# One copy instead of six of the logit and gate columns in a routed two-layer kernel

## The chip, the cores and the metric

The kernel runs on one core of one Trainium2 chip. The metric is the time of one execution on the device in microseconds (us). The engines are named as the profile names them: PE is TensorE, PEld its weight loads, DVE is VectorE, ACT is ScalarE, POOL is GpSimd and SP is SyncE, which issues most of the transfers.

## The reference

A gated scan over 4 x 5056 tokens of 256 features comes first, then two mixture-of-experts layers with 8 experts of width 1024. Layer 1 has a skip score for every token.

```python
f = lower_bound + (1 - lower_bound) * sigmoid(f_logit)
h = f[:, t] * h + (1 - f[:, t]) * x[:, t]            # the scan; its outputs are the tokens x
logits = x @ w_gate                                  # 8 columns for each layer
e = argmax(logits); g = softmax(logits)[e]
y = g * (relu(x @ w1[e]) @ w2[e])                    # for the tokens of expert e
out = x + y where x @ w_skip > 0, else x             # layer 1
out = y                                              # layer 2, on layer 1's output
```

## The kernel before

**Stages.** The 20224 tokens are cut into 40 chunks of 512 (the last is shorter), and each chunk into tiles of 128. For each chunk the kernel loads x and f (lines 818 to 829), makes the gates on ACT (lines 834 and 839), scans on DVE (lines 844 and 856), transposes the result back to rows on PE (line 880, copied out of PSUM by ACT at line 883), computes the logits (function `logits`, from line 894), routes, ranks, and scatters the rows into a region for each expert in DRAM. From the 17th chunk on (I0 = 16) units of up to 256 tokens of layer 1 run in between, four steps to a chunk: two products (lines 609 and 637 to 639) with the results split in two float16 halves by ACT (line 620) and DVE (line 621). When the scan is through, the remaining units of layer 1 and then those of layer 2 follow, one after the other.

**The logits.** One matrix `wgt` of 17 columns holds both layers' gates and the skip vector. For the first 20 chunks (CF = 20) `logits` multiplies in float32: for each of 4 tiles and each of 2 halves of the features, the transposed tokens are the stationary operand, loaded anew each time, and `wgt17` is the moving one. `wgt17` is `wgt` read RG times over through a broadcast view, so that a product streams 6 x 17 = 102 columns and fills 102 columns of PSUM; only the first 17 are read afterwards, by ACT at line 916. Later chunks use float16 halves with 34 and 17 columns (lines 923 and 926) and no copies.

**The gate products.** Layer 1's second weights are extended by 8 columns, the product of the expert's `w2` with layer 2's gate. `wsplit` transposes a quarter of a weight on PE (line 1029, copied out by ACT at line 1030), and `gate_product` (line 1032) makes 4 x 2 float32 products with the transposed quarter stationary and `wgt8`, 8 columns read RG times, moving: 48 columns, of which 8 are read by ACT and DVE in `w_split` (lines 184 and 185). There are 16 such batches (8 experts, two quarters each), and they all lie in the first 127 us. The same function is called in `reload`, which belongs to a loop for units left over at the end.

**What sets the order.** Each engine's order is written out by hand: `side(k)` calls `work`, `weights` and the unit steps slot by slot, and PE, DVE, ACT, POOL and SP keep that order. In the trace a float32 product is two matmul instructions, so a batch of logits for one chunk and a batch of gate products for one quarter are 16 each; a transpose is one. The logits of a chunk go to PSUM tiles that they share with the transposes of line 880 (pool `pt`, 2 buffers of one size for all), so that a batch waits for ACT's copy at line 883.

Of the kernel before, what the change touches and what calls it, by code (L numbers as in the profile page):

```python
# [56 lines left out]

WB, LT, LT2, UW = 2, 6, 5, 4

RG = 6  # L60
CLG, CTOK, CGATE = D, D + E, D + E + 1
W = 272

# [31 lines left out]
def moe_chain(ctx: ExitStack, tc: tile.TileContext, xT, fT, lb, wg, w1a, w2a, w1b, w2b, out):  # L95
# [74 lines left out]

    wgt17 = wgt.unsqueeze(2).broadcast_to([P, 2, RG, 17])
    wgt8 = wgt[:, :, :E].unsqueeze(2).broadcast_to([P, 2, RG, E])

# [568 lines left out]
    with ExitStack() as ph:  # L742
# [152 lines left out]
        def logits(c):  # L895
# [8 lines left out]
            if c < CF:  # L904
                psl = pt.tile([P, CJ, RG, 17], F32, tag="px", name="ps_l")
                for j in range(n):
# [125 lines left out]
        def gate_product(wT):  # L1032

            psv = pm.tile([P, 4, RG, E], F32, tag="pm", name="ps_v")
            for f in range(4):
# [485 lines left out]
```

## Time and profile before

| | us |
|---|---|
| median of 3 runs | 1583.88 |
| lowest and highest | 1580.51 and 1587.67 |
| profiled execution | 1587.33 |
| its span, first to last instruction | 1585.6 |
| PE busy in it | 1498.6 (95%) |
| DVE busy, ACT busy | 925.5 (58%), 725.0 (46%) |
| mean granted PE clock | 0.979 |

Busy shares are averages over stages with different limits, so the stretches are to be read one by one. The granted clock stands beside each stretch: 1.00 is 2.4 GHz and 0.50 is 1.2 GHz; a value in between is a mean over a stretch with both. In the timeline an instruction's own time is longer than the distance to the next, since matmuls are pipelined: the pace is read from the starts.

### The profile page before, as it was taken

The numbers are of one execution on the slowest core, as the hardware profiler recorded it, in microseconds if no ns is written. First come the engines' busy times: TensorE is split into PE (matmuls) and PEld (weight loads), VectorE is DVE, ScalarE is ACT, GpSimd is POOL, SyncE is SP. The second block draws the span as 40 slices with busy tenths as digits, with TensorE's granted clock in tenths as the row PEclk, the third lists the DMA queues.
The fourth block names the chain that finished last, engine by engine and source line by source line (L and its number), as shares of the span: only waits on it lengthen the run. The fifth ranks groups of instructions, "written<-read, shape, count | busy, mean of one in ns | idle before, by whom it ended". The sixth has DMA issues, their size and how long they took to land. (4 is left out here: it accounts for less than half of the span.)

```text
span 1585.6 us, 41240 instructions
## 1 busy us (share of the span) xinstructions
PE 1498.6 (95%) x13900; PEld 1346.4 (85%) x13901; DVE 925.5 (58%) x1947; ACT 725.0 (46%) x1419; POOL 507.9 (32%) x511
## 2 busy tenths in 40 slices
PE   5878989999999998999999999999999999999996
PEld 5877868888988887887888998998989989989985
DVE  5877677888885865546755555544444444444442
ACT  6777567776763232333344443433333333333332
POOL 1663455646453177016111111111111111111121
PEclk9988989999999999999999999999999999999998
DMA  8876655777774377327333323111111111111110
GB/s 289 274 266 212 212 178 201 260 243 252 242 253 153 103 232 244 121 71 243 110 100 103 97 98 106 50 49 56 49 50 57 47 51 50 49 54 49 49 48 22
DMA packets 127221, 213.73 MB, mean 135 GB/s; under 512 B 14459, under 2 KB 87807, under 8 KB 124464
## 3 DMA queue, kind: packets, MB, share of 16 engines
q1 hardware_dynamic: 107824, 157.51, 31.5%
q0 software_dynamic: 19200, 53.53, 9.2%
q8 instruction: 132, 2.16, 0.6%
q14 instruction: 65, 0.53, 0.1%
HBM read 120.10 MB, written 70.80 MB: 120 GB/s over the span
## 5 line engine op out<-in xcount | busy, mean ns | idle before, releaser
L621 DVE SCALAR_TENSOR_TENSOR hl<-ps_m,hh 128x512 f16<-128x512 f32 (+1 forms) x504 | 336.9, 668 | 554.6 <-ACT hh L620 553.1
L620 ACT ACTIVATE hh<-ps_m 128x512 f16<-128x512 f32 (+1 forms) x504 | 292.2, 580 | 634.8 <-PE ps_m L609 527.3
L637 PE MATMUL ps_o<-wt,hh 128*128 (+2 forms) x1936 | 531.7, 275 | 8.4 <-DVE rows L645 8.4
L638 PE MATMUL ps_o<-wt,hh 128*128 (+2 forms) x1936 | 531.8, 275 | 0.0
L639 PE MATMUL ps_o<-wt,hl 128*128 (+2 forms) x1936 | 531.7, 275 | 0.0
L609 PE MATMUL ps_m<-xh,w1s 128*128 128x256 f16 (+1 forms) x2880 | 505.9, 267 | 0.0
L609 PEld LDWEIGHTS <-w1s 128*128 128x128 f16 x4320 | 406.7, 98 | 45.5 <-issue 0.4
L274 POOL DMA_INDIRECT out_dram<-rows,dest x162 | 157.6, 973 | 750.1 <-ACT rows L681 636.8
L609 PE MATMUL ps_m<-xl,w1s 128*128 128x256 f16 (+1 forms) x1440 | 378.6, 267 | 0.0
L638 PEld LDWEIGHTS <-hh 128*128 128x128 f16 x1936 | 190.0, 98 | 33.5 <-issue 9.3
L609 PE MATMUL ps_m<-xh,wt 128*128 128x256 f16 x1152 | 215.9, 276 | 2.4 <-DVE hl L621 2.4
L639 PEld LDWEIGHTS <-hl 128*128 128x128 f16 x1936 | 190.1, 98 | 25.0
L637 PEld LDWEIGHTS <-hh 128*128 128x128 f16 x1936 | 190.0, 98 | 22.6
L274 POOL DMA_INDIRECT regions<-rw,dest x158 | 175.9, 1113 | 91.9 <-issue 42.5
L609 PEld LDWEIGHTS <-wt 128*128 128x128 f16 x1728 | 168.8, 99 | 23.8 <-issue 3.1
L609 PE MATMUL ps_m<-xl,wt 128*128 128x256 f16 x576 | 158.7, 276 | 0.0
L583 DVE COPY w1s<-wt 128x4096 f16 x90 | 110.8, 1231 | 11.6 <-issue 4.8
L274 POOL DMA_INDIRECT regions<-wt,b_dest x80 | 84.7, 1059 | 42.2 <-issue 17.9
L856 DVE TENSOR_TENSOR_SCAN xt<-ft,end,xt 128x512 f32<-128x512 f32 (+4 forms) x78 | 94.9, 1246 | 0.4
L598 DVE SCALAR_TENSOR_TENSOR xl<-ps_x,xh 128x512 f16<-128x512 f32 (+1 forms) x126 | 83.1, 660 | 16.7 <-ACT xh L597 16.6
L596 PE MATMUL ps_x<-ident,rows 128*128 128x128 f32 x484 | 75.0, 276 | 18.2 <-DMA rows<-regions 18.2
L681 ACT ACTIVATE rows<-ps_o,rows 128x256 f32<-128x256 f32 x162 | 68.3, 471 | 33.2 <-PE ps_o L639 33.2
(241 smaller groups left out, 1317.1 us busy)
## 6 DMA issues: line engine op xcount, KB each, us to landing
rows<-regions SPq DMA_DIRECT2D x116, 272.0 KB, 2.8
wt<-wt SPq DMA_DIRECT2D x20, 1024.0 KB, 6.0
ft<-in_fT_dram SPq DMA_DIRECT2D x39, 512.0 KB, 4.0
xt<-in_xT_dram SPq DMA_DIRECT2D x39, 512.0 KB, 4.9
wt<-mid SPq DMA_DIRECT2D x40, 272.0 KB, 4.5
mid<-rows SPq DMA_DIRECT2D x38, 272.0 KB, 3.6
wt<-in_w2a_dram SPq DMA_DIRECT2D x16, 512.0 KB, 4.7
wt<-in_w1a_dram SPq DMA_DIRECT2D x16, 512.0 KB, 3.9
```

The source lines that it names most:

```text
L274: r = nc.gpsimd.indirect_dma_start(out=dst, out_offset=bass.IndirectOffsetOnAxis(ap=idx_ap, axis=0), in_=rows_ap, in_offset=None, bounds_c ...
L583: nc.vector.tensor_copy(t.w1, wt[:, bass.ds(o, W2O)])
L596: nc.tensor.transpose(ps[:, d, j * P : (j + 1) * P], t.rows[:, j, d * P : (d + 1) * P], ident)
L598: nc.vector.scalar_tensor_tensor(out=t.xl, in0=ps, scalar=SX, in1=t.xh, op0=ALU.mult, op1=ALU.subtract)
L609: nc.tensor.matmul(ps[:, f, :], lhsT=t.w1[:, wo : wo + P], rhs=x[:, d, :], start=f == 0 and k == 0, stop=f == 1 and k == 5, skip_group_che ...
L620: nc.scalar.activation(hh, ps, AF.Relu)
L621: nc.vector.scalar_tensor_tensor(out=hl, in0=ps, scalar=0.0, in1=hh, op0=ALU.max, op1=ALU.subtract)
L637: nc.tensor.matmul(ps, lhsT=hh[:, f, js], rhs=hi, start=first, stop=False)
L638: nc.tensor.matmul(ps, lhsT=hh[:, f, js], rhs=lo, start=False, stop=False)
L639: nc.tensor.matmul(ps, lhsT=hl[:, f, js], rhs=hi, start=False, stop=last)
L681: nc.scalar.activation(y, t.ps[j][:, :D], AF.Copy, scale=t.rows[:, j, CGATE : CGATE + 1])
L856: nc.vector.tensor_tensor_scan(x[:, d, s0:s1], f[:, d, s0:s1], x[:, d, s0:s1], init, ALU.mult, ALU.subtract)
```

## The change

RG falls from 6 to 1. The broadcast views then hold one copy: each logits product of the first 20 chunks streams 17 columns instead of 102, and each gate product 8 instead of 48. The number of matmuls, of weight loads, of copies out of PSUM and of transfers stays as it is, and so do the results, since the five further copies were never read. The PSUM tiles shrink with RG, inside pools whose buffers are sized by other tiles.

```diff
-RG = 6
+RG = 1
 CLG, CTOK, CGATE = D, D + E, D + E + 1
```

The lines that read RG, unchanged:

```python
wgt17 = wgt.unsqueeze(2).broadcast_to([P, 2, RG, 17])            # line 171
wgt8 = wgt[:, :, :E].unsqueeze(2).broadcast_to([P, 2, RG, E])    # line 172
psl = pt.tile([P, CJ, RG, 17], F32, tag="px", name="ps_l")       # line 905
psv = pm.tile([P, 4, RG, E], F32, tag="pm", name="ps_v")         # line 1034
```

## Rows read from the trace of the kernel before

**Rows 1.** Windows by stage: busy us (instructions) per engine, granted clock, DMA share.

```profile
14.64:143.11 128.47, 104.97 (x792) 100.22 (x792) 100.41 (x200) 96.90 (x204) 64.58 (x62) 0.86 0.81 270
143.11:240.00 96.89, 85.12 (x754) 75.14 (x754) 70.08 (x136) 60.70 (x111) 48.38 (x38) 0.94 0.57 187
240.00:480.00 240.00, 234.86 (x2392) 209.65 (x2391) 195.14 (x468) 170.16 (x327) 131.41 (x110) 1.00 0.70 240
...
800.00:1200.00 400.00, 400.00 (x3667) 360.15 (x3665) 196.89 (x285) 155.04 (x277) 70.01 (x72) 1.00 0.24 75
```

**Rows 2.** Groups by line, PE, 14.64 to 143.11 us: busy, mean ns, idle before.

```profile
L1037 PE MATMUL ps_v<-wgt,wt 128*128 128x48 f32 x256 | 35.6, 299 | 2.2 <-ACT wt L1030 2.2
L908 PE MATMUL ps_l<-wgt,xt 128*128 128x102 f32 x224 | 34.4, 316 | 15.3 <-ACT rw L883 15.3
L1029 PE MATMUL ps_w<-ident,wt 128*128 128x128 f32 x128 | 19.9, 307 | 0.0
L880 PE MATMUL ps_t<-ident,xt 128*128 128x128 f32 x113 | 18.0, 304 | 3.9 <-ACT rw L883 2.5 <-DVE xt L856 1.3
...
L225 PE MATMUL ps_rank<-oh,ones 128*128 128x112 f16 (+6 forms) x42 | 2.3, 192 | 0.0
```

**Rows 3.** Timeline, PE, 66 to 73 us: start, length, instructions merged by batch.

```profile
67.24 1.06 PE L1029 MATMUL ps_w<-ident,wt 128*128 128x128 f32 x8
68.13 1.93 PE L908 MATMUL ps_l<-wgt,xt 128*128 128x102 f32 x16
69.90 0.22 PE L222 MATMUL ps_rank<-oh,ltri 128*128 128x128 f16 x1
...
70.24 1.93 PE L1037 MATMUL ps_v<-wgt,wt 128*128 128x48 f32 x16
72.02 1.05 PE L1029 MATMUL ps_w<-ident,wt 128*128 128x128 f32 x8
```

**Rows 4.** Timeline, PE, 110 to 122 us.

```profile
110.47 3.74 PE L908 MATMUL ps_l<-wgt,xt 128*128 128x102 f32 x16 [1.02 <-ACT rw L883]
114.00 3.53 PE L1037 MATMUL ps_v<-wgt,wt 128*128 128x48 f32 x16
117.33 1.93 PE L1029 MATMUL ps_w<-ident,wt 128*128 128x128 f32 x8
119.05 1.51 PE L880 MATMUL ps_t<-ident,xt 128*128 128x128 f32 x8
120.40 1.88 PE L1037 MATMUL ps_v<-wgt,wt 128*128 128x48 f32 x16
```

**Rows 5.** Windows by batch, columns as in rows 1 (PE first, clock third last).

```profile
22.62:24.42 1.80, 1.80 (x16) 1.80 (x17) 1.12 (x1) 1.13 (x2) 0.00 (x0) 1.00 1.10 366
24.52:27.86 3.34, 3.34 (x19) 3.34 (x17) 2.71 (x5) 1.49 (x5) 0.00 (x1) 0.50 1.06 399
27.86:31.20 3.34, 3.34 (x17) 3.23 (x17) 2.10 (x6) 3.28 (x8) 0.22 (x1) 0.50 1.05 373
31.49:33.35 1.86, 1.86 (x16) 1.86 (x17) 1.77 (x6) 1.86 (x3) 0.00 (x0) 1.00 0.35 105
...
92.70:96.00 3.30, 3.30 (x18) 3.30 (x17) 3.10 (x5) 2.71 (x4) 2.59 (x2) 0.50 0.69 245
96.45:98.19 1.74, 1.74 (x19) 1.74 (x17) 1.29 (x6) 1.39 (x5) 0.46 (x2) 1.00 0.77 262
```

**Rows 6.** Windows from one logits batch to the next, columns as in rows 1.

```profile
41.12:49.10 7.98, 5.54 (x51) 5.31 (x50) 6.69 (x17) 6.66 (x16) 6.50 (x6) 1.00 0.83 249
...
110.47:123.01 12.54, 12.54 (x72) 12.54 (x73) 8.33 (x23) 7.55 (x17) 6.74 (x7) 0.62 0.74 246
```

**Rows 7.** Waits of ACT, 110.47 to 123.01 us: total us, times, longest.

```profile
ACT ls L916 <- PE ps_l L908: 2.9, 1, 2.9
```

**Rows 8.** Timeline, PE, 253 to 258 us: logits of a later chunk, in float16.

```profile
254.26 0.18 PE L923 MATMUL ps_l<-wg,ft 128*128 128x34 f16 x1 [0.51 <-ACT rw L883]
254.28 0.17 PE L926 MATMUL ps_l<-wg,ft 128*128 128x17 f16 x1
```

## The prediction

> **What bounds the kernel now.** I read the windows by stage first, then PE's groups in the one stage that the change touches, then PE's timeline there with the granted clock beside it. The windows [rows 1] show three regimes. From 240 us on PE is busy 234.86 of 240.00 us and later 400.00 of 400.00 us at full clock: its own order of work sets the end. From 143 to 240 us it is busy 85.12 of 96.89 us. In the first stage, 14.64 to 143.11 us, no engine is: PE 104.97, DVE 100.41, ACT 96.90 of 128.47 us, and the clock averages 0.86. Each engine's order is fixed and the units of layer 1 stand in PE's order behind this stage's work, so a microsecond that the first stage loses or gains reaches the end nearly whole, as PE has hardly an idle stretch later in which to make it up.
>
> All 256 instructions of the gate products and 224 of the logits (14 batches of 16) lie in that stage [rows 2]; the other 6 batches of logits stand after 143 us among dense float16 products.
>
> **What a narrow product costs PE.** The change removes 85 of 102 moving columns from a logits product and 40 of 48 from a gate product, and no instruction. The pace is read from the starts at full clock [rows 3]: 16 logits instructions take 69.90 - 68.13 = 1.77 us, 16 gate products 72.02 - 70.24 = 1.78 us, 8 transposes 68.13 - 67.24 = 0.89 us. That is 0.111 us an instruction for 102, 48 and 128 columns alike, so columns don't set it; each instruction has its own float32 stationary operand, and that is what these batches have in common. At half clock [rows 4] it is the same picture: 3.53 us, 3.33 us and 1.72 us, so 0.221, 0.208 and 0.215 us each. Taking 48 columns as the nearest row to 17 and 8, the removed columns save nothing on the pace. From both sides: at most the pace of a float16 product of 17 columns, which comes 0.02 us after the one before it [rows 8] (a far row with other operands; it is a rival below), and no loss, since in no row fewer columns take longer. What is saved besides is the end of a batch's last matmul: 102 columns against 48 are 316 against 299 ns in the mean [rows 2], so some 0.03 us in each of 30 batches, 1 us if all of it is waited for. ACT and DVE read the same 17 and 8 columns at another stride: nothing, with either sign too small for a row. PSUM buffers, transfers and queues are untouched, and no wait is added.
>
> **What it costs in clock.** What the removed columns did do is keep PE occupied. The windows by batch [rows 5] show what PE did before each change of level. At 22.62 us 16 logits run at 1.00 after a pause, and the clock is 0.50 from 24.5 us on. The next batch, 16 gate products without a gap, keeps PE busy 3.34 of 3.34 us and the clock stays at 0.50. Then 16 transposes of 128 columns run, equally without a gap, and from 31.49 us it is 1.00. The same order stands at 110.47 us [rows 4]: logits and gate products of 102 and 48 columns run at half for 6.86 us, 16 transposes follow, and at 120.40 us the next gate products start at the full pace. At 92.70 us a batch nearly all of logits ran at 0.50, and the next products were at 1.00 [rows 5]. So with PE equally busy, batches of 128 columns raised the clock, batches of 102 did once and once didn't, batches of 48 didn't. With 17 and 8 columns I expect that logits and gate products never raise it and that each run of them lets it fall; only runs of transposes raise it.
>
> The Trainium skill ("TensorE: Matmul & The Clock Gate", Part 1, What's actually happening) says that a monitor sets the clock by how busy PE has lately been. Read as the time that PE is busy, that rule would leave this change without any effect; the gate products at 0.50 with PE busy throughout [rows 5] speak against that reading.
>
> **The sum.** PE's work in the first stage, at either level. Full [rows 2, 3]: 256 x 0.111 + 224 x 0.111 + (128 + 113) x 0.111 = 80 us, and 6 rank batches of 70.24 - 69.90 = 0.34 us, a dozen products of the first unit and 4 transposes for 3 us more: 83 us. Half [rows 2, 4]: 256 x 0.208 + 224 x 0.221 + 241 x 0.215 = 155 us, and twice 3 us: 161 us. Today the stage takes 128.47 us, 104.97 us of it busy, so PE waits 23.5 us, mostly for ACT's copy out of PSUM before a logits batch (15.3 us [rows 2]).
>
> How much of the waiting stays: at full clock a turn from one batch of logits to the next takes 7.98 us with 5.54 us busy; a turn with a second batch of gate products (72 instructions for 51) at a mean of 0.62 takes 12.54 us, all of it busy [rows 6]. So a slow PE becomes the bound of its turn, ACT and DVE are covered by it, and ACT waits for PE instead (2.9 us in that turn, for the logits [rows 7]; the extension's copies and the transposes' copies stand behind it on ACT, and behind these the next logits). Bounds for the idle time that stays: 0 and 23.5 us. I take half, 12 us, since the stretches at full clock and the start of the stage keep theirs.
>
> Which share is at full: a turn holds one run of logits and, for most, gate products, then up to 16 transposes on end. Such a run lasts 3.5 us at half; I take it that it raises the clock by its end or shortly before, and that the next narrow run takes it away again. That leaves about 2 us in turns of some 10 to 11 us, a fifth at full, a mean clock of 0.60. The stage then takes 83 / 0.60 + 12 = 150 us, 22 us more than 128.47. Ends: half of the time at full, mean 0.75, with 12 us idle gives 123 us, no loss at all; a third at full, mean 0.67, gives 136 us, +8; everything at half gives 161 us without and 185 us with today's idle time, +33 to +56.
>
> After 143 us nothing changes: the 6 batches of logits there stand between products of 256 columns at 0.94 and 1.00 [rows 1], which are dense without them. The first unit's products at 140 us may start at half for a little longer (under 2 us, as today's batches at half cost twice), which I set against the 1 us saved above. Of the 22 us all reaches the end. On the profiled execution (1587.33 us, 1.7 us around a span of 1585.6) that is 1609; it lay 3.45 us above the median, so the forecast is 1584 + 22 = **1606 us**.
>
> **Rivals.** *The clock holds as today.* If transposes alone raise it, as before 31.49 and 120.40 us [rows 4, 5], and pauses alone lower it, PE runs the same pace at the same levels: 1584 us, within 8 us of before. For it: the pauses before logits at full clock are real (15.3 us in all [rows 2]), and falls follow them. Against it: the rise before 96.45 us, with logits ahead of it [rows 5]. Chance 0.12.
>
> *Nothing raises it.* The whole stage runs at half: 161 to 185 us, the middle 173, +44, so 1628 us. For it: where a turn has a second batch of gate products, these stand between its transposes. Against it: the two rises behind 16 transposes on end. Chance 0.15. The Trainium skill (the same page, Part 4: PE-mode transpose) says that transposes don't count as PE being busy in the same way; by that rule this rival would be the forecast, with its 1628 us. The rises after runs of transposes alone [rows 4, 5] disagree with it.
>
> *Columns are the pace after all.* If narrow float32 products came as fast as the float16 ones, 0.02 us instead of 0.111 [rows 8], PE would save about 480 x 0.09 = 43 us of its busy time in the first stage, and ACT would set the turns: its 96.90 us and some waiting, about 112 us, -16, so 1568 us. Its place is the 30 batches, and it decides if 16 narrow products at full clock take under about 1.2 us. Against it: 48 and 102 columns differ by 0.01 us in 16. Chance 0.04.
>
> **How the numbers follow.** The forecast, a clock that is at half for most of the first stage and raised by transposes only, has 0.69, from +8 to +33 us: 1592 to 1617. The clock as today 0.12, half throughout 0.15 (1617 to 1640), columns as the pace 0.04. The range takes the forecast's own and most of half throughout, 1589 to 1630; outside it lie most of the first rival, the third, and the upper end of the second, some 0.2 in all. A measurement of this kernel can tell about 0.5%, 8 us, from no change. Slower by more: 0.69 and 0.15, less a little for forecasts that end low, 0.83. Within: 0.13. Faster: 0.04.
>
> **What would show it.** In the changed kernel's windows the first stage's clock should be near 0.60 instead of 0.86, the stage some 20 us longer with PE busy over 90% of it, and everything after it the same length, moved. PE's timeline should still show 16 logits in 1.8 us at full and 3.3 to 3.5 us at half; ACT's waits for line 908 and 1037 should grow while PE's waits for line 883 shrink. I am wrong if the clock stays at 0.8 or more there, if 16 narrow products take clearly less than 3.3 us at half, or if the stage grows and the end doesn't.

## The result: 1.1% slower, all of it lost in the first stage

| | before | after |
|---|---|---|
| median of 6 runs, us | 1584.85 | 1602.63 |
| lowest and highest, us | 1579.92, 1587.67 | 1596.04, 1608.45 |
| ratio, with its 95% interval | 1 | 1.0106 [1.0074, 1.0139] |
| span of the profiled execution, us | 1585.6 | 1599.9 |
| first to fifteenth batch of logits ("the first stage"), us | 128.5 | 143.9 |
| from there to the end of the span, us | 1442.5 | 1441.5 |

The first stage is 15.4 us longer, the rest of the profiled execution 1.0 us shorter. The windows by stage of the changed kernel show it (columns: stretch, us, then PE, PEld, DVE, ACT and POOL busy with instructions, granted clock, DMA share, GB/s); rows 1 answer to them.

```profile
14.50:158.36 143.86, 136.05 (x792) 131.81 (x792) 100.54 (x200) 98.23 (x204) 65.12 (x62) 0.67 0.72 242
158.36:255.00 96.64, 88.58 (x757) 77.81 (x757) 70.43 (x138) 60.98 (x112) 47.86 (x38) 0.91 0.56 187
255.00:495.00 240.00, 235.07 (x2393) 209.56 (x2391) 195.30 (x466) 170.14 (x327) 131.33 (x110) 1.00 0.70 240
...
815.00:1215.00 400.00, 400.00 (x3666) 360.16 (x3665) 197.10 (x285) 154.54 (x276) 70.01 (x72) 1.00 0.24 75
33.30:158.36 125.06, 118.80 (x713) 115.02 (x712) 88.72 (x179) 85.99 (x180) 64.66 (x60) 0.62 0.68 229
```

PE has the same 792 instructions there and is busy 136.05 us instead of 104.97 us; DVE and ACT are busy as long as before. One thing must be known to read the clock column: until the trace's first clock record, here at 33.3 us, it shows 1.00, though the pace says half (16 logits in 17.94 - 14.50 = 3.44 us). So the last row begins there: 0.62, against 0.86 in before from 33 us to the end of its first stage (that row stands with the experiments).

The groups by line of PE in the first stage (busy, mean ns of one, idle time before them), which answer to rows 2:

```profile
L1037 PE MATMUL ps_v<-wgt,wt 128*128 128x8 f32 x256 | 46.2, 318 | 0.0
L908 PE MATMUL ps_l<-wgt,xt 128*128 128x17 f32 x224 | 37.6, 314 | 5.4 <-ACT rw L883 5.4
L1029 PE MATMUL ps_w<-ident,wt 128*128 128x128 f32 x128 | 29.0, 402 | 0.0
L880 PE MATMUL ps_t<-ident,xt 128*128 128x128 f32 x113 | 26.5, 409 | 2.4 <-ACT rw L883 2.4
```

The gate products have a sixth of their columns and take 46.2 us instead of 35.6. The transposes, of which the change touches nothing, take 29.0 + 26.5 = 55.5 us instead of 19.9 + 18.0 = 37.9. Work that was not edited grew by nearly half: that is a clock, not the cost of an instruction.

PE's timeline of the changed kernel, its pace at either level (answers to rows 3 and 4):

```profile
14.50 3.60 PE L908 MATMUL ps_l<-wgt,xt 128*128 128x17 f32 x16
17.94 1.95 PE L1029 MATMUL ps_w<-ident,wt 128*128 128x128 f32 x8
...
96.31 1.96 PE L908 MATMUL ps_l<-wgt,xt 128*128 128x17 f32 x16 [1.02 <-ACT rw L883]
98.11 0.26 PE L222 MATMUL ps_rank<-oh,ltri 128*128 128x128 f16 x1
...
98.66 3.53 PE L1037 MATMUL ps_v<-wgt,wt 128*128 128x8 f32 x16
102.04 1.95 PE L1029 MATMUL ps_w<-ident,wt 128*128 128x128 f32 x8
103.78 1.63 PE L880 MATMUL ps_t<-ident,xt 128*128 128x128 f32 x8
105.24 1.85 PE L1037 MATMUL ps_v<-wgt,wt 128*128 128x8 f32 x16
106.95 0.31 PE L1029 MATMUL ps_w<-ident,wt 128*128 128x128 f32 x1
```

At full clock 16 products of 17 columns take 98.11 - 96.31 = 1.80 us and 16 of 8 columns 106.95 - 105.24 = 1.71 us; at half 3.44 us and 102.04 - 98.66 = 3.38 us. With 102 and 48 columns it was 1.77 and 1.78 us, 3.53 and 3.33 us. The removed columns saved PE at most 0.07 us in a batch of 16.

### The profile page after: what moved, and what is told of

It is laid out like the page before. It is cut to its first block, busy times and chain, and to the rows that moved or that the text cites. A ratio compares the mean times of both kernels' runs of the same rounds, so it can differ in the third digit from the quotient of the medians.

```text
span 1599.9 us, 41241 instructions
## 1 busy us (share of the span) xinstructions
PE 1533.4 (96%) x13900; PEld 1380.4 (86%) x13901; DVE 926.1 (58%) x1947; ACT 726.3 (45%) x1419; POOL 507.7 (32%) x511
## 5 line engine op out<-in xcount | busy, mean ns | idle before, releaser
L681 ACT ACTIVATE rows<-ps_o,rows 128x256 f32<-128x256 f32 x162 | 68.3, 471 | 33.3 <-PE ps_o L639 32.9
```

Source lines behind the costliest of these rows:

```text
L681: nc.scalar.activation(y, t.ps[j][:, :D], AF.Copy, scale=t.rows[:, j, CGATE : CGATE + 1])
```

## The experiments

Two theories stood against each other at first: the clock (narrow products leave PE too little occupied, and it runs at half for longer) and the edit's other effect, a smaller PSUM tile that ACT and DVE read at another stride; further on, that narrow products cost time by themselves. Each kernel ran beside the kernel before on one chip, and chips differ by 2%, so ratios are compared, not times. The stage and the clock are those of one profiled execution each, and executions of one kernel differ, so a few microseconds of a stage decide nothing.

| kernel | ratio to before [95%] | first stage, us | clock from 33 us to its end |
|---|---|---|---|
| before | 1 | 128.5 | 0.86 |
| the changed kernel, again | 1.0125 [1.0092, 1.0158] | 145.1 | 0.60 |
| one copy, old PSUM layout | 1.0142 [1.0092, 1.0192] | 145.9 | 0.59 |
| three copies | 1.0066 [1.0040, 1.0093] | 144.1 | 0.64 |
| logits one, gates six | 1.0046 [1.0021, 1.0071] | 133.2 | 0.72 |
| logits six, gates one | 1.0022 [0.9990, 1.0054] | 138.2 | 0.76 |
| one copy, float16 products between | 1.0016 [0.9993, 1.0039] | 135.7 | 0.83 |
| logits seven, gates sixteen | 0.9970 [0.9947, 0.9993] | 127.4 | 0.91 |
| the same, and products in the pauses | 0.9958 [0.9932, 0.9984] | 124.9 | 0.97 |
| one copy, products between and in the pauses | 0.9960 [0.9934, 0.9985] | 128.5 | 0.94 |

The windows from 33 us to the end of the first stage that the last column is read from. The length of the stretch comes before the comma, PE's busy time behind it, the clock third last.

Before:

```profile
33.00:143.11 110.11, 89.24 (x700) 85.31 (x700) 87.77 (x179) 83.28 (x177) 64.12 (x60) 0.86 0.78 259
```

The changed kernel, again:

```profile
33.00:159.67 126.67, 122.47 (x711) 118.82 (x711) 88.66 (x179) 86.17 (x179) 61.48 (x60) 0.60 0.68 225
```

One copy in the old PSUM layout:

```profile
33.00:160.57 127.57, 123.03 (x700) 119.78 (x699) 87.82 (x179) 85.22 (x177) 61.22 (x60) 0.59 0.67 224
```

Three copies:

```profile
33.00:158.53 125.53, 116.84 (x714) 112.57 (x712) 88.68 (x179) 86.46 (x180) 61.45 (x60) 0.64 0.70 228
```

Logits one, gates six:

```profile
33.00:147.42 114.42, 102.44 (x709) 98.52 (x709) 88.61 (x179) 85.07 (x179) 64.71 (x60) 0.72 0.75 251
```

Logits six, gates one:

```profile
33.00:152.53 119.53, 102.33 (x702) 98.67 (x702) 88.26 (x179) 84.32 (x177) 62.73 (x60) 0.76 0.71 239
```

One copy, float16 products between:

```profile
33.00:149.94 116.94, 98.05 (x922) 94.50 (x922) 88.66 (x179) 85.08 (x178) 63.65 (x60) 0.83 0.76 247
```

Logits seven, gates sixteen:

```profile
33.00:141.89 108.89, 84.94 (x702) 80.31 (x700) 87.60 (x179) 83.12 (x177) 72.62 (x60) 0.91 0.79 264
```

The same, and products in the pauses:

```profile
33.00:141.23 108.23, 92.81 (x831) 87.32 (x829) 87.29 (x179) 82.94 (x177) 65.81 (x60) 0.97 0.79 264
```

One copy, products between and in the pauses:

```profile
33.00:145.26 112.26, 100.89 (x1042) 95.87 (x1042) 87.69 (x179) 83.33 (x177) 66.38 (x60) 0.94 0.78 256
```

**One copy in the old layout.** The matmuls write one copy; the tiles keep six.

```diff
-RG = 6
+RG = 1
-psl = pt.tile([P, CJ, RG, 17], F32, tag="px", name="ps_l")
+psl = pt.tile([P, CJ, 6, 17], F32, tag="px", name="ps_l")
-                            psl[:, j],
+                            psl[:, j, :RG],
...
```

> One copy is computed, but the PSUM tiles keep their room for six, so ACT and DVE read at the old stride. Clock theory: nothing but the moving columns matters, so it runs as the changed kernel: 1603 us (+18), the first stage (first logits batch to the fifteenth) 142 to 146 us, its clock 0.6 to 0.7. Rival, layout (the narrower PSUM tile is read or shared differently): as before, 1585 us, the stage 128 us.

Measured: 1.0142, the stage 145.9 us, the clock 0.59 (0.62 over the whole stage), as the changed kernel on another chip. With the old layout the loss is all there: the layout and the stride are not the cause.

**Each part alone.**

```diff
-RG = 6
+RL, RE = 1, 6
```

RL counts the copies of the logits' columns, RE those of the gate products'; the second run has 6 and 1.

> Only the logits are computed once; the gate products keep six copies (48 columns). Clock theory: the logits, the wider of the two, carry most of the loss, since the clock of the kernel before never rose behind gate products alone: +10 to +14 us, the first stage 138 to 143 us. Rival, equal shares (each narrow batch costs alike, 14 batches to 16): +8 us. Rival, the clock holds and something else costs: no number, but then the stage's clock stays at 0.86.

> Only the gate products are computed once; the logits keep six copies (102 columns). Clock theory: runs of logits and transposes still raise the clock or keep it, runs of gate products let it fall a little more often than before: +3 to +8 us, the first stage 131 to 137 us. Rival, equal shares: +9 us.

Measured: 1.0046 with narrow logits, +7 us of 1612, and 1.0022 with narrow gate products, +4 us and not surely above nothing. The first expectation of +10 to +14 us was a miss. That logits carry more of it than gate products is not shown either: the intervals overlap, and the stages of the profiled executions came out the other way round, 133.2 us with narrow logits (138 to 143 expected) and 138.2 us with narrow gate products (131 to 137 expected).

Do the two parts add up? By the ratios they fall short of the whole: 0.46% and 0.22% alone, 1.06 to 1.42% together. A reason for that lies in the windows: before, PE stands idle for 20.9 us of the stretch (110.11 - 89.24), with one part narrow still for 12 us (114.42 - 102.44) and 17 us (119.53 - 102.33), with both for 4.5 us (127.57 - 123.03), so part of a slower PE falls into time in which it waited anyway, and with both narrow little of that time is left. But these runs don't show that the parts don't add. The sum of the two has an interval of its own, some 0.3 to 1.1% if their errors are independent, which overlaps with each interval of the whole; the medians on this chip lie 9.7 and 5.8 us above before for the parts and 16.8 us for both; and the stages are 4.7 and 9.7 us longer than before's for the parts and 15.4 to 17.4 us for both.

**Three copies.** 51 and 24 columns.

```diff
-RG = 6
+RL, RE = 3, 3
```

> Three copies for both (51 and 24 columns). Clock theory: the loss goes with the columns that stream, so it lies between one and six copies and nearer to one, since 48 columns raised nothing in the kernel before: 1.005 to 1.011 of before, the first stage 135 to 142 us. Rival, only the very narrow products are bad (a fixed cost of short matmuls): within 1.003.

> The changed kernel itself, for comparison with the others on the same chip. From the first result 1.0106 and from the layout experiment 1.0142 of the time of before: 1.009 to 1.016; the first stage 142 to 147 us, its clock from 33 us on 0.58 to 0.65.

Measured: 1.0066 with three, between the 1.0125 of one copy on the same chip and before, as the clock theory has it; the rival's limit of 1.003 is outside the interval. The stage of its profiled execution, 144.1 us, is longer than expected; that execution took 1599.88 us, the longest of its ten, whose median is 1593.82. One copy came out as expected.

**Work added beside narrow products.** One copy, and behind each narrow product a float16 product of ones, 256 columns wide, into columns of the same PSUM tile that nobody reads (`psw` is that tile, now 512 columns wide).

```diff
                            rhs=wgt17[:, d],
                            ...
                        )
+                        nc.tensor.matmul(
+                            psw[:, 256:].rearrange("p (a b) -> p a b", a=2), lhsT=ones,
+                            rhs=ones.unsqueeze(1).broadcast_to([P, 2, P]),
+                            start=False, stop=False, skip_group_check=True,
+                        )
```

> One copy, as in the changed kernel, and behind each of the 8 narrow products of every batch one float16 product of ones with 256 columns into unread columns of the same PSUM tile: 288 more matmuls, 31 us more of streaming at full clock if none of it overlapped. Clock theory: PE is occupied again, the clock of the first stage returns to 0.85 or more and the kernel is faster than the changed one in spite of the added work: 1580 to 1592 us, the first stage 125 to 135 us. Rival, the narrow products cost time by themselves: slower than the changed kernel, 1605 to 1630 us, the clock below 0.7.

Measured: 1.0016. PE has 288 matmuls more than in the changed kernel and the kernel is about 1% faster than with one copy alone; the clock is 0.83 where 0.85 or more was expected, the stage 135.7 us where at most 135 was. Its timeline at full clock, the first and the last of a gate batch's products:

```profile
66.70 0.29 PE L1043 MATMUL ps_v<-wgt,wt 128*128 128x8 f32 x2
66.84 0.27 PE L1051 MATMUL ps_v<-ones 128*128 128x256 f16 x1
66.95 0.28 PE L1043 MATMUL ps_v<-wgt,wt 128*128 128x8 f32 x2
...
68.58 0.27 PE L1051 MATMUL ps_v<-ones 128*128 128x256 f16 x1
68.69 1.03 PE L1034 MATMUL ps_w<-ident,wt 128*128 128x128 f32 x8
```

The batch takes 68.69 - 66.70 = 1.99 us with its 8 additions and 1.71 us without, 0.035 us for each.

**Wider than before.** Seven copies of the logits and sixteen of the gate products, as many as their PSUM tiles hold.

```diff
-RG = 6
+RL, RE = 7, 16
```

> More copies than before: seven of the logits (119 columns) and sixteen of the gate products (128 columns, as the transposes have). The pace of the products is set by the loads of their stationary operands, so the wider ones cost no time. Clock theory: batches of gate products now raise the clock as transposes do, and only pauses lower it; from 33 us on the clock is 0.90 or more instead of 0.86, the first stage 118 to 126 us, 0.993 to 0.998 of before. Rival, columns cost time on PE: 1.000 or more, the paces over 0.12 us an instruction at full clock.

```profile
41.21 1.94 PE L908 MATMUL ps_l<-wgt,xt 128*128 128x119 f32 x16
42.99 1.96 PE L1037 MATMUL ps_v<-wgt,wt 128*128 128x128 f32 x16
44.79 1.03 PE L1029 MATMUL ps_w<-ident,wt 128*128 128x128 f32 x8
```

Measured: 0.9970, faster than before. Its timeline shows 1.78 us for 16 products of 119 columns and 1.80 us for 16 of 128, so from 8 to 128 columns the pace is the same. The clock is 0.91, as expected; the stage of 127.4 us is a little longer than I had expected.

**The pauses filled.** The same, and 12 unread float16 products ahead of the logits of chunks 0 to 13, where PE waits for ACT.

```diff
+                if c < I0 - 2:
+                    psf = po.tile([P, 512], F32, tag="po", name="ps_f")
+                    for i in range(12):
+                        nc.tensor.matmul(
+                            psf[:, :256].rearrange("p (a b) -> p a b", a=2), lhsT=ones,
+                            rhs=ones.unsqueeze(1).broadcast_to([P, 2, P]), start=i == 0, stop=i == 11,
+                        )
```

> As the experiment with more copies, and 12 float16 products of ones with 256 columns into an unread PSUM tile ahead of the logits of chunks 0 to 13, where PE waits for ACT in a turn at full clock: 1.3 us of work in a pause of 2 to 2.7 us. Clock theory: the pauses no longer lower the clock, 0.95 or more from 33 us on, the first stage 112 to 122 us, 0.990 to 0.997 of before. Rival, the stage is bound by ACT and DVE at full clock or the added products delay the logits: no faster than with more copies alone.

Measured: 0.9958, faster than both kernels. The clock is at 0.97, yet the stage is 124.9 us and not 112 to 122. Even that is flattered: the added products stand ahead of the first batch of logits too, which starts at 16.29 instead of 14.54 us, and the stage ends only 0.7 us earlier than with more copies alone (141.23 against 141.89 us). So the clock is hardly what bounds it any more, and against more copies alone the gain lies inside the intervals: the rival's part of this holds. In the window DVE and ACT are busy 87.29 and 82.94 of 108.23 us, as in every other kernel here.

**Narrow, with both additions.**

> One copy of the columns, as in the changed kernel, with both additions: a float16 product of ones behind each narrow product, and 12 of them in the pause ahead of the logits of chunks 0 to 13. PE has 456 matmuls more than the changed kernel. Clock theory: nothing in narrow products themselves costs time, so with the clock held up the kernel is as fast as with wide ones: 0.95 or more from 33 us on, the first stage 122 to 130 us, 0.995 to 1.001 of before. Rival, narrow products cost something beside the clock: slower than before, 1.004 or more, with the clock over 0.9.

Measured: 0.9960, with the columns computed once, beside 0.9958 with wide columns and the same products in the pauses. The clock, 0.94, falls just short of the 0.95 expected. The stage alone doesn't show the gain: it is 128.5 us, and before was not profiled on this chip. But over whole executions the granted clock was 0.981 to 0.989 with these additions and 0.968 to 0.982 before. So narrow products as such cost no time that these runs can tell; the clock that they let fall did.

## Why the prediction was right

The range held the time and the forecast, 22 us more, stands against 17.8 us between the medians. Step by step:

- **The pace of a narrow product** was right: 1.71 to 1.80 us for 16 at full clock with 8, 17, 119 and 128 columns.
- **What lowers and raises the clock** was right in the main. In the changed kernel the transposes are nearly all that still is wide in this stage, and the clock rose with them: each of its eight rises there stands within 0.7 us of the end of a run of 16 transposes. With narrow products that raise nothing, the Trainium skill's rule that transposes don't count as PE being busy in the same way ("TensorE: Matmul & The Clock Gate", Part 4: PE-mode transpose) would have left the whole stage at half, and the trace disagrees. Not each run of 16 did it, though: four of the twelve didn't. The timeline has two runs:

```profile
38.02 1.95 PE L1029 MATMUL ps_w<-ident,wt 128*128 128x128 f32 x8
39.76 1.91 PE L880 MATMUL ps_t<-ident,xt 128*128 128x128 f32 x8
41.47 3.42 PE L1037 MATMUL ps_v<-wgt,wt 128*128 128x8 f32 x16
...
53.17 1.95 PE L1029 MATMUL ps_w<-ident,wt 128*128 128x128 f32 x8
54.91 1.91 PE L880 MATMUL ps_t<-ident,xt 128*128 128x128 f32 x8
56.70 2.18 PE L908 MATMUL ps_l<-wgt,xt 128*128 128x17 f32 x16
```

Behind the first run the gate products went on at half (44.74 - 41.47 = 3.27 us for 16), behind the second the logits came at about the full pace (58.73 - 56.70 = 2.03 us). The windows around them, and a later one:

```profile
36.80:57.00 20.20, 20.20 (x97) 19.92 (x96) 11.85 (x27) 12.64 (x26) 9.21 (x9) 0.50 0.63 210
57.30:60.50 3.20, 3.20 (x38) 3.20 (x37) 3.08 (x3) 2.07 (x6) 0.45 (x1) 1.00 0.46 164
...
105.10:111.70 6.60, 6.60 (x62) 6.60 (x61) 5.06 (x7) 5.48 (x13) 3.76 (x4) 1.00 0.67 229
```

  For 20.20 us PE was busy without a gap, and the clock stayed at 1.2 GHz. That is the plainest case against reading the Trainium skill's rule that the clock goes by how busy PE has lately been ("TensorE: Matmul & The Clock Gate", Part 1, What's actually happening) as the time that PE is busy. Nor did each narrow run lower the clock, which I had expected: from 105.10 to 111.70 us two batches of gate products and one of logits ran at full before it fell.
- **The share at full** was a guess of a fifth, a mean of 0.60; it is 0.62 from 33.3 us on and half before, which makes (18.8 x 0.5 + 125.06 x 0.62) / 143.86 = 0.60 for the stage. That the mean was hit is luck. I had some 2 us at full in every turn (the stretch from one batch of logits to the next); in fact some turns have none and others more than half, as the rows below show. Busy time was forecast at 138 us and is 136.05.
- **The idle time that stays** was mis-sized: 12 us forecast, 143.86 - 136.05 = 7.8 us measured. It makes 4.2 of the 6.1 us by which the stage was forecast too long. The turns say where it stands, first to last (rows 6 show before's):

```profile
14.50:23.15 8.65, 7.10 (x34) 6.69 (x33) 4.91 (x4) 5.93 (x13) 0.24 (x1) 1.00 1.03 329
...
46.48:56.70 10.22, 10.22 (x49) 9.94 (x48) 4.30 (x16) 6.08 (x15) 4.20 (x5) 0.50 0.64 210
...
88.09:96.30 8.21, 7.19 (x49) 6.95 (x48) 6.40 (x14) 6.29 (x15) 4.74 (x4) 0.79 0.51 162
...
146.99:158.36 11.37, 9.00 (x40) 7.56 (x41) 9.79 (x21) 7.14 (x15) 8.35 (x8) 0.50 0.84 303
```

  A turn at half that has gate products has no idle time at all. Half of what is left stands in the first turn (8.65 - 7.10 = 1.55 us; its clock column is from before the first record, its pace is that of half) and in the last (11.37 - 9.00 = 2.37 us), which run at half and have no gate products; nearly all the rest stands in turns with a piece at full, about 1 us in each of four. Half of the old idle time was too much.
- **Who waits for PE**: PE's waits for ACT's copy at line 883 shrank, as I had said: ahead of the logits from 15.3 us (rows 2) to 5.4 us. For the other side I named ACT behind logits and gate products. Its waits for the logits grew from 6.0 to 7.6 us over the stage, and it doesn't wait for the gate products in either trace; the larger growth is behind the transposed weights, which stand behind the gate products on PE. Waits of ACT in the first stage, before and after:

```profile
ACT ls L916 <- PE ps_l L908: 6.0, 4, 2.9
ACT wt L1030 <- PE ps_w L1029: 1.7, 2, 1.4
```

```profile
ACT wt L1030 <- PE ps_w L1029: 12.8, 15, 2.4
ACT ls L916 <- PE ps_l L908: 7.6, 4, 2.7
```

- **After the stage** I allowed under 2 us for the first unit. The first 8 us behind the stage ran at half, to 166.4 us, and by the sixteenth batch of logits the loss had grown by 174.88 - 158.36 - (156.22 - 143.11) = 3.4 us; by the twentieth (235.37 against 220.08 us) it was back at 15.3. That all of the stage's loss reaches the end fits: the rest took 1441.5 us against 1442.5, and the medians are 17.8 us apart. One pair of executions shows it only roughly: of the kernels with the old layout, with each part alone and with products between, all on one chip, what follows the stage took from 1459.8 to 1472.1 us.
- **The rivals.** The clock held as today: no, 0.62. Nothing raises it: no, it rose behind transposes. Columns as the pace: no.

Left open: which part of the 36 us that the kernel before spends at half in its first stage (2 x 0.14 x 128.47 us) the pauses cause and which its narrower gate products. And why a run of 16 transposes raised the clock in one place and not in another is not settled by these runs.

## What to carry to other kernels

Columns that nobody reads can be worth their place: where each product loads its own stationary operand, more columns cost PE nothing here, up to 128, and fewer can cost the clock for all that runs on PE beside them. Before such columns are taken out, look at the granted clock of the stage and at what PE did before each change of level, and price unedited work in it at the lower level. And look at PE's idle time: a slower clock can hide in it (12 and 17 us are left with one part narrow) and shows when it is used up (4.5 us with both). Whether two such changes together cost more than their sum isn't settled here.

## What I had not expected of the hardware

A float16 product of 256 columns between float32 products with operands of their own lengthened the batch by 0.035 us, where float16 products of 256 columns come 0.11 us apart in the dense part of the kernel (line 609, starts at 254.66 and 254.77 us in the trace of before). That most of it runs beside the loads of the other operands is my reading; no run separates it. And work that computes nothing made the kernel faster: 456 unread products more than in the changed kernel, and 1.0125 became 0.9960.
